# Outputs wait in the weights' staging buffers, stores go behind the loads, and the order is made anew

## The chip, the cores and the metric

The kernel runs on one core of a Trainium2 chip. The metric is the time of one execution on the device, in microseconds (us), as the median of several runs.

## The reference

Attention with a sliding window of 128 positions and 4 sink positions, for 4 batches of 8 heads, 768 positions and 64 channels a head; then a channel mix with a token shift over the 512 channels.

```python
scores = scale * np.matmul(q, k.transpose(0, 1, 3, 2))
keep = is_sink | in_window            # position < 4, or 0 <= row - column < 128
a = softmax(np.where(keep, scores, -1e9))
x = (a @ v).transpose(0, 2, 1, 3).reshape(B, S, 512)
x_prev = x shifted by one position, zeros first
xk = mu_k * x + (1 - mu_k) * x_prev
xr = mu_r * x + (1 - mu_r) * x_prev
k = np.maximum(xk @ w_k, 0)           # 512 -> 1024
out = sigmoid(xr @ w_r) * ((k * k) @ w_v)
```

## The kernel before

The 4 x 768 positions are cut into 12 blocks (u = 0 to 11) of 256 positions, three to a batch. For each block the kernel prepares q and k, attends, mixes, and runs the channel mix of the block.

- `load` brings q, k and v of a block in halves of 256 KB into three staging buffers each (`ks`, `qs`, `vs`). `load_weight` brings the five 1 MB pieces of the weights (two of w_k, one of w_r, two of w_v) into three staging buffers `w32`; in the traces their name is `w`. `cast` turns them into bfloat16 (`wk_sb`, `wr_sb`, `wv_h`).
- `prepare` casts q and k to bfloat16 (`qb`, `kb`, L533 and L540) and turns them: for early blocks by transposes on PE (L573) and an evacuation into `qt` and `kt` (L586), for later blocks by transposing DMAs (L559). v is cast into `vb` (L643).
- `attend` makes scores on PE (L718), exponentials on ACT (L772), a multiplication by the mask on DVE (L786), the products with v on PE (L805), and a reciprocal and a multiplication on DVE (L819, L822) into `x`.
- `mix` transposes `x` (L846 on PE with an evacuation at L855, or DMAs at L866 for the last blocks) into `xt`, and makes the differences `td` (L874) and the pieces of `xk` and `xr` (L885), four of each for a block, on DVE.
- `ffn` makes the key products on PE (L936, 32 for a block, which need all four pieces of `xk`), relu and square (L946 to L964), the gate (L976, L982), the value products (L994), the output `ob` on DVE (L1003) and its store (L1010).

No loop sets the order at run time. Each step is an operation with a number; the table `ORDER` lists the numbers in the order in which they are emitted, `CHOICE` says for some of them which of ACT, DVE and POOL does it, and `SLOTS` gives the place in its pool to each result. Every engine then works through its own instructions in that order, and waits where a result or a place is missing. All transfers of consequence are issued on SP's queue, in order too. A negative number in `ORDER` is a filler product on PE (L1014), which nobody reads.

Finished outputs wait in `ob`, a pool of three places, until SP has stored them.

Of the kernel before, what the change touches and what calls it, by code (L numbers as in the profile page):

```python
# [18 lines left out]
    90: "ACT", 91: "ACT", 92: "ACT", 93: "ACT", 95: "ACT", 97: "ACT", 99: "ACT", 100: "DVE",  # L19
    103: "DVE", 108: "DVE", 109: "POOL", 111: "DVE", 112: "ACT", 113: "ACT", 139: "DVE", 142:  # L20
    "DVE", 144: "DVE", 145: "DVE", 148: "DVE", 151: "DVE", 154: "DVE", 196: "POOL", 199: "POOL",
    202: "POOL", 206: "DVE", 223: "DVE", 227: "DVE", 228: "ACT", 278: "DVE", 283: "DVE", 284:
    "POOL", 287: "ACT", 288: "DVE", 300: "DVE", 309: "ACT", 313: "ACT", 320: "DVE", 356: "DVE",
    358: "POOL", 363: "POOL", 366: "ACT", 367: "ACT", 369: "DVE", 389: "ACT", 446: "DVE", 447:
    "ACT", 527: "DVE", 548: "ACT", 552: "ACT", 555: "DVE", 560: "ACT", 595: "DVE", 597: "DVE",
    600: "POOL", 602: "DVE", 605: "ACT", 606: "DVE", 628: "ACT", 636: "ACT", 677: "POOL", 681:
    "DVE", 683: "DVE", 684: "DVE", 702: "ACT", 706: "ACT", 710: "ACT", 714: "ACT", 753: "DVE",
    759: "DVE", 761: "ACT", 782: "DVE", 783: "ACT", 787: "ACT", 791: "ACT", 795: "ACT", 832:
    "DVE", 838: "ACT", 839: "ACT", 859: "ACT", 866: "DVE", 867: "ACT", 906: "POOL", 912: "DVE",
    914: "ACT", 915: "DVE", 931: "ACT", 935: "ACT", 939: "ACT", 943: "ACT", 1000: "DVE", 1004:  # L30
    "DVE", 1005: "ACT", 1008: "DVE", 1009: "ACT", 1028: "DVE", 1037: "ACT",
# [116 lines left out]
class Plan:  # L148
# [23 lines left out]
    def run(self):  # L172
        keys = [(name, key) for o in self.ops for name, key in o["take"]]
        for (name, key), slot in zip(keys, SLOTS, strict=True):
            self.buf[key] = self.pools[name][slot]
# [8 lines left out]
def kernel(  # L184
# [14 lines left out]
    nc = tc.nc  # L199
# [7 lines left out]
    NC = Dm // 128  # L207
# [6 lines left out]
    P = Plan()  # L214
# [164 lines left out]
    warm = tile1([128, 256], BF16, "warm")  # L379
# [689 lines left out]
```

## Time and profile before

| | us |
|---|---|
| median of 3 runs | 169.1 |
| lowest, highest | 167.48, 170.65 |
| the profiled execution, span | 167.6 |

The page and the trace are of one execution, whose span from first to last instruction is 167.6 us; that is near the lowest of the runs. The granted clock of PE is 1.00 in nearly all of it.

In the tables a row of a timeline is: start in us, time to the end in us, engine, source line, operation, out<-in, shapes, how many were merged; in square brackets the engine's idle time before it and what ended it. Instructions of one engine overlap at their ends, so the time of a step in a full stream is read from start to start. A row of waits is: who waited, for what, us in total, how often, the longest. Line numbers of the changed kernel are three to seven higher at the same place.

### The profile page before, as it was taken

Reading aid. Unit: us, or ns where it says so; the run is one execution under the profiler, and the core shown is the slowest. Engines: PE = TensorE matmul, PEld = TensorE weight load, DVE = VectorE, ACT = ScalarE, POOL = GpSimd, SP = SyncE. Lnnn points to the kernel's source line nnn. Section 1 sums busy time; section 2 is a strip of 40 time slices with the busy share of each in tenths; the row PEclk is TensorE's granted clock in tenths of the full one; section 3 lists DMA queues with packets and bytes.
Section 4 is the critical chain, followed back from the end, with each engine's and each line's share of the span. In section 5 each row is a group of like instructions: output and inputs, shape, how many; then the busy total and the mean of one; then the engine's idle time right before and its main releaser. Section 6 shows DMA issues by size and latency. Waiting matters only on the chain.

```text
span 167.6 us, 4210 instructions
## 1 busy us (share of the span) xinstructions
PE 159.7 (95%) x1601; PEld 102.4 (61%) x1601; DVE 146.2 (87%) x375; ACT 133.4 (80%) x221; POOL 16.6 (10%) x43
## 2 busy tenths in 40 slices
PE   6999997999999999899999999999999999999991
PEld 1447574755558576676556885665765576764850
DVE  5189999999999999899999999989798799998821
ACT  4269998999999997999879999989799829614340
POOL 6423021005000010022000000010010000000000
PEclk9999999999999999999999999999999999999999
DMA  4999989999899999979999999999997774131303
GB/s 102 300 327 369 346 172 312 372 324 328 189 248 166 204 294 224 253 153 133 218 256 149 214 239 174 233 219 200 211 189 185 194 162 155 63 66 63 125 0 125
DMA packets 79042, 34.60 MB, mean 206 GB/s; under 512 B 67112, under 2 KB 73520, under 8 KB 79024
## 3 DMA queue, kind: packets, MB, share of 16 engines
q1 hardware_dynamic: 79008, 34.35, 92.0%
q8 instruction: 12, 0.20, 0.5%
q14 instruction: 6, 0.05, 0.1%
q10 hardware_dynamic: 16, 0.00, 0.0%
HBM read 24.12 MB, written 6.29 MB: 181 GB/s over the span
## 4 chain that ended last, share of the span: by engine, by line
PE 58%; DVE 11%; DMA 11%; SPq 7%; ACT 7%; issue 3%; ACTq 0%; DVEq 0%
PE bank L936 18%; PE bank L994 18%; PE bank L976 8%; DMA vs<-in_v_dram 6%; SPq L334 5%; PE sc L718 4%; PE bank L805 4%; DMA qs<-in_q_dram 3%; ACT e L772 3%; DMA qt<-qb 2%; DVE ob L1003 2%; DVE e L786 2%; PE bank L846 2%; DVE x L822 2%; PE bank L573 2%
## 5 line engine op out<-in xcount | busy, mean ns | idle before, releaser
L936 PE MATMUL bank<-xk,wk_sb 128*128 128x256 bf16 x384 | 48.1, 273 | 0.1
L994 PE MATMUL bank<-wv_h,kk 128*128 128x512 bf16 x184 | 46.4, 379 | 0.0
L772 ACT ACTIVATE e<-sc 128x1024 bf16<-128x1024 f32 (+1 forms) x48 | 45.4, 974 | 1.2 <-PE sc L718 1.2
L936 PEld LDWEIGHTS <-wk_sb 128*128 128x128 bf16 x384 | 36.2, 98 | 7.6 <-issue 0.7
L786 DVE TENSOR_TENSOR e<-e,mask 128x1024 bf16<-128x1024 bf16 (+1 forms) x48 | 30.7, 655 | 0.7 <-ACT e L772 0.5
L946 ACT ACTIVATE rl<-bank 128x512 bf16<-128x512 f32 x38 | 22.4, 616 | 8.6 <-PE bank L936 8.5
L994 PEld LDWEIGHTS <-kk 128*128 128x128 bf16 x184 | 16.6, 98 | 14.4 <-issue 0.3
L976 PE MATMUL bank<-wr_sb,xr 128*128 128x512 bf16 x96 | 23.8, 379 | 0.0
L885 DVE SCALAR_TENSOR_TENSOR xr<-td,mu_all,xt 128x256 bf16<-128x256 bf16 x48 | 22.5, 482 | 0.0
L885 DVE SCALAR_TENSOR_TENSOR xk<-td,mu_all,xt 128x256 bf16<-128x256 bf16 x48 | 21.3, 477 | 0.1
L964 ACT ACTIVATE kk<-rl 128x512 bf16<-128x512 bf16 x26 | 16.7, 649 | 5.3 <-DVE rl L950 5.3
L822 DVE TENSOR_TENSOR x<-bank,rec 128x256 bf16<-128x256 f32 x48 | 19.2, 416 | 0.3
L1003 DVE SCALAR_TENSOR_TENSOR ob<-th,bank 128x512 f32<-128x512 f32 x23 | 15.7, 681 | 4.2 <-PE bank L994 3.3
L805 PEld LDWEIGHTS <-e 128*128 128x128 bf16 x352 | 14.4, 97 | 5.8 <-DVE e L786 1.0
L805 PE MATMUL bank<-vb,e 128*128 128x65 bf16 x352 | 16.9, 193 | 0.8 <-DVE e L786 0.8
L982 ACT ACTIVATE th<-bank 128x512 f32<-128x512 f32 x24 | 14.3, 616 | 3.6 <-PE bank L976 3.5
L1014 PE MATMUL bank<-warm 128*128 128x512 bf16 x44 | 13.8, 440 | 1.5 <-DVE warm L1032 1.1
L718 PE MATMUL sc<-qt,kt 64*128 64x128 bf16 (+1 forms) x256 | 13.9, 237 | 0.3 <-DMA qt<-qb 0.2
L976 PEld LDWEIGHTS <-xr 128*128 128x128 bf16 x96 | 8.9, 98 | 8.6
L718 PEld LDWEIGHTS <-kt 64*128 64x128 bf16 x256 | 9.3, 94 | 4.5 <-issue 3.0
L874 DVE TENSOR_TENSOR td<-xt 128x512 bf16<-128x512 bf16 x24 | 10.1, 425 | 0.8 <-ACT xt L855 0.8
L855 ACT COPY xt<-bank 128x512 bf16<-128x512 bf16 x15 | 9.1, 608 | 1.8 <-PE bank L846 1.8
(72 smaller groups left out, 157.9 us busy)
## 6 DMA issues: line engine op xcount, KB each, us to landing
vs<-in_v_dram SPq DMA_DIRECT2D x24, 256.0 KB, 5.0
ks<-in_k_dram SPq DMA_DIRECT2D x24, 256.0 KB, 5.6
qs<-in_q_dram SPq DMA_DIRECT2D x24, 256.0 KB, 5.1
out_dram<-ob SPq DMA_DIRECT2D x23, 256.0 KB, 2.9
w<-in_moe_w_k_dram SPq DMA_DIRECT2D x2, 1024.0 KB, 7.3
w<-in_moe_w_v_dram SPq DMA_DIRECT2D x2, 1024.0 KB, 8.6
w<-in_moe_w_r_dram SPq DMA_DIRECT2D x1, 1024.0 KB, 7.1
kt<-kb SPq DMA_TRANSPOSE x16, 4.1
```

Source lines behind the costliest of these rows:

```text
L718: nc.tensor.matmul(out=sc[:, a, o0:o1], lhsT=lhs[rows], rhs=rhs[rows], start=u not in BIAS, stop=True, skip_group_check=u in BIAS)
L772: nc.scalar.activation(out=buf[ek][:, :, lo:], in_=buf[sck][:, :, lo:], func=AF.Exp, scale=scale)
L786: nc.vector.tensor_tensor(out=at, in0=at, in1=m, op=ALU.mult)
L805: nc.tensor.matmul(out=o[:, g, a, :], lhsT=e[:, a, e0:e0 + 128], rhs=rhs, start=(T == 0 and i == 0), stop=(i == len(blocks) - 1), skip_gro ...
L822: P.op("DVE", dve(256), lambda ok=ok, rk=rk, c=c: nc.vector.tensor_tensor(out=buf["x", u][:, :, 128 * c:128 * c + 128].rearrange("p g (a d ...
L885: nc.vector.scalar_tensor_tensor(out=buf[key][:, c, :], in0=buf[tk][:, i, :], scalar=mu[w][:, c:c + 1], in1=xt[:, c, t0 - 1:t0 + 255], op0 ...
L936: nc.tensor.matmul(out=ps[:, i, :], lhsT=wk_sb[:, c, 128 * f:128 * f + 128], rhs=xk[:, c, :], start=(c == 0), stop=(c == NC - 1), skip_gro ...
L946: nc.scalar.activation(out=buf[rk], in_=buf[psk].rearrange("p (i t) -> p i t", i=2), func=AF.Relu)
L964: nc.scalar.activation(out=buf["kk", u][:, 2 * f2:2 * f2 + 2, :], in_=buf[rk], func=AF.Square)
L976: nc.tensor.matmul(out=buf[psk], lhsT=buf["xr", u][:, c, 128 * g:128 * g + 128], rhs=wr_sb[:, c, :], start=(c == 0), stop=(c == NC - 1))
L994: nc.tensor.matmul(out=buf[psk], rhs=wv_h[:, f, :], lhsT=buf["kk", u][:, f, 128 * g:128 * g + 128], start=(f == 0), stop=(f == NF - 1))
L1003: P.op("DVE", dve(512), lambda psk=psk, tk=tk, bk=bk: nc.vector.scalar_tensor_tensor(out=buf[bk], in0=buf[tk], scalar=1.0, in1=buf[psk], o ...
```

## The change

- The pool `ob` gets the twelve quarters of the three weight staging buffers as further places, 15 in all. In the traces an output in such a place is called `w`.
- `ORDER`, `CHOICE` and `SLOTS` are new. A filler product may have 128 columns, which the new order does not use.

```diff
+    P.pools["ob"] += [w[:, c, :] for w in P.pools["w32"] for c in range(NC)]
...
-                self.fill(self.pools["bank"][-1 - i])
+                self.fill(banks[(-1 - i) % len(banks)], 512 if -i <= len(banks) else 128)
...
 CHOICE = {
-    90: "ACT", 91: "ACT", 92: "ACT", 93: "ACT", 95: "ACT", 97: "ACT", 99: "ACT", 100: "DVE",
+    90: "POOL", 91: "POOL", 92: "POOL", 93: "POOL", 94: "POOL", 95: "POOL", 96: "ACT", 98:
...
 ORDER = (
-    4, 80, 77, 0, 81, 79, 78, 82, 1, 2, 85, 3, 112, 84, 8, -1, -2, -3, -4, -1, -2, 88, 83, 6,
+    80, 82, 83, 85, 0, 2, 77, 78, 1, 79, 100, 106, -1, -2, -3, -4, -1, -2, 88, -2, -3, -4, -2,
```

Counted over the whole program, DVE has 351 instructions instead of 375, ACT 207 instead of 222, POOL 82 instead of 43, PE 34 filler products instead of 44; all other products are the same.

The first place is SP's queue from its start to the key weights `w_76` and `w_77`, before:

```order
L304 DMA vs_73<-in_v_dram 128x8x64
L334 DMA ks_67<-in_k_dram 64x4x256 x2
L334 DMA qs_70<-in_q_dram 64x4x256 x2
L334 DMA qs_71<-in_q_dram 64x4x256
L334 DMA ks_68<-in_k_dram 64x4x256 x2
L334 DMA qs_71<-in_q_dram 64x4x256
L334 DMA qs_72<-in_q_dram 64x4x256
L304 DMA vs_73<-in_v_dram 128x8x64
L334 DMA qs_72<-in_q_dram 64x4x256
L351 DMA w_76<-in_moe_w_k_dram 128x4x512
L334 DMA ks_69<-in_k_dram 64x4x256
L351 DMA w_77<-in_moe_w_k_dram 128x4x512
```

and now (the buffers 67 to 69 are `ks`, 70 to 72 `qs`, 73 to 75 `vs`):

```order
L338 DMA qs_71<-in_q_dram 64x4x256 x2
L338 DMA ks_68<-in_k_dram 64x4x256 x2
L308 DMA vs_73<-in_v_dram 128x8x64 x2
L308 DMA vs_74<-in_v_dram 128x8x64
L338 DMA ks_69<-in_k_dram 64x4x256 x2
L338 DMA qs_72<-in_q_dram 64x4x256 x2
L308 DMA vs_74<-in_v_dram 128x8x64
L338 DMA ks_67<-in_k_dram 64x4x256 x2
L338 DMA qs_70<-in_q_dram 64x4x256 x2
L355 DMA w_76<-in_moe_w_k_dram 128x4x512
L355 DMA w_77<-in_moe_w_k_dram 128x4x512
```

Ahead of these rows now stand the four halves of `ks_67` and `qs_70` for block 0. The loads of q and k for blocks 0 to 3 and of v for blocks 0 and 1 stand ahead of the weights, where before the first weights came after 12 loads.

The second place is DVE ahead of the last piece of `xk_113`, block 0's. Before, from the reciprocal of the last attention step of block 0:

```order
L819 RECIPROCAL rec_104<-bank_63 128x4
L874 TENSOR_TENSOR td_110<-xt_155 128x512
L822 TENSOR_TENSOR x_107<-bank_63,rec_104 128x2x128
L786 TENSOR_TENSOR e_94<-e_94,mask 128x1024
L885 TENSOR_SCALAR xr_117<-td_110,mu_all,xt_155 128x256
L885 TENSOR_SCALAR xk_113<-td_110,mu_all,xt_155 128x256
L874 TENSOR_TENSOR td_111<-xt_155 128x512
L885 TENSOR_SCALAR xk_113<-td_110,mu_all,xt_155 128x256
L885 TENSOR_SCALAR xk_113<-td_111,mu_all,xt_155 128x256 x2
```

and now the end of that stretch (`x_108` is block 1's attention):

```order
L823 RECIPROCAL rec_103<-bank_66 128x4
L826 TENSOR_TENSOR x_108<-bank_64,rec_106 128x2x128
L889 TENSOR_SCALAR xk_113<-td_110,mu_all,xt_155 128x256
L826 TENSOR_TENSOR x_108<-bank_66,rec_103 128x2x128
L878 TENSOR_TENSOR td_111<-xt_155 128x512
L826 TENSOR_TENSOR x_108<-bank_65,rec_102 128x2x128
L889 TENSOR_SCALAR xk_113<-td_110,mu_all,xt_155 128x256
L878 TENSOR_TENSOR td_112<-xt_155 128x512
L889 TENSOR_SCALAR xk_113<-td_111,mu_all,xt_155 128x256 x2
```

Block 1's masks, reciprocals and all four `x_108` have moved ahead of block 0's last piece; two of its evacuations and two casts for later blocks stand there as well.

The third place is SP's queue around the last load. Before, the stores stood among the loads; now the rows from the first store on are:

```order
L1014 DMA out_dram<-ob_133 128x512
L563 DMA_TRANSPOSE qt_92<-qb_82 128x4x128
L308 DMA vs_75<-in_v_dram 128x8x64
L563 DMA_TRANSPOSE qt_92<-qb_82 128x4x128
L308 DMA vs_74<-in_v_dram 128x8x64
L870 DMA_TRANSPOSE xt_156<-x_107 128x4x128 x2
L1014 DMA out_dram<-w_76 128x512
L563 DMA_TRANSPOSE kt_85<-kb_81 128x4x128 x2
L1014 DMA out_dram<-w_78 128x512
L870 DMA_TRANSPOSE xt_156<-x_108 128x4x128 x2
L1014 DMA out_dram<-ob_134 128x512
L1014 DMA out_dram<-w_76 128x512
```

One store of 25 stands ahead of the last load (`vs_74`) where there were 15, and the rest follow it.

More of the change, by code (lines that the diff above doesn't have):

```diff
@@ L18 @@
 CHOICE = {
-    90: "ACT", 91: "ACT", 92: "ACT", 93: "ACT", 95: "ACT", 97: "ACT", 99: "ACT", 100: "DVE",
[L20 to L30, printed above, removed]
@@ L31 @@
-    "DVE", 1005: "ACT", 1008: "DVE", 1009: "ACT", 1028: "DVE", 1037: "ACT",
+    90: "POOL", 91: "POOL", 92: "POOL", 93: "POOL", 94: "POOL", 95: "POOL", 96: "ACT", 98:
+    "ACT", 99: "ACT", 100: "DVE", 103: "DVE", 106: "POOL", 108: "DVE", 109: "POOL", 113: "DVE",
+    139: "POOL", 142: "POOL", 144: "DVE", 145: "POOL", 147: "DVE", 148: "POOL", 150: "DVE", 193:
+    "DVE", 196: "POOL", 198: "DVE", 202: "DVE", 224: "ACT", 228: "ACT", 232: "ACT", 235: "DVE",
+    278: "DVE", 280: "DVE", 284: "DVE", 287: "ACT", 288: "ACT", 293: "DVE", 300: "DVE", 309:
@@ new lines @@
+    "ACT", 316: "DVE", 356: "POOL", 358: "POOL", 361: "POOL", 363: "POOL", 367: "ACT", 385:
+    "ACT", 389: "ACT", 393: "ACT", 397: "ACT", 438: "POOL", 441: "POOL", 443: "POOL", 456:
+    "DVE", 464: "DVE", 465: "ACT", 473: "ACT", 516: "POOL", 518: "POOL", 521: "POOL", 523:
+    "POOL", 526: "ACT", 548: "ACT", 560: "ACT", 595: "POOL", 597: "POOL", 600: "POOL", 602:
+    "POOL", 628: "ACT", 636: "ACT", 675: "POOL", 683: "DVE", 701: "DVE", 702: "ACT", 706: "ACT",
+    710: "ACT", 714: "ACT", 753: "POOL", 757: "POOL", 759: "POOL", 774: "DVE", 783: "ACT", 791:
@@ L32 @@
+    "ACT", 795: "ACT", 830: "POOL", 834: "DVE", 836: "POOL", 838: "DVE", 855: "ACT", 859: "ACT",
+    863: "ACT", 906: "DVE", 910: "POOL", 912: "POOL", 931: "ACT", 935: "ACT", 943: "ACT", 996:
+    "DVE", 997: "ACT", 1001: "ACT", 1009: "ACT", 1025: "ACT", 1029: "ACT", 1033: "ACT", 1036:
+    "DVE",
 }
@@ L175, in run @@
             self.buf[key] = self.pools[name][slot]
+        banks = self.pools["bank"]
         for i in ORDER:
             if i < 0:
-                self.fill(self.pools["bank"][-1 - i])
+                self.fill(banks[(-1 - i) % len(banks)], 512 if -i <= len(banks) else 128)
             else:
@@ L1012, in ffn, with zeros @@
             P.op("SP", 400.0, store, rank, hold=[bk], reads=[bk], service=800.0)
-    P.fill = lambda bank: nc.tensor.matmul(out=bank, lhsT=warm[:, 0:128], start=True,
-                                           rhs=warm.unsqueeze(1).to_broadcast([128, 2, 256]),
-                                           stop=True)
+    def zeros(bank, n):
+        nc.tensor.matmul(out=bank[:, 0:n], lhsT=warm[:, 0:128], start=True, stop=True,
+                         rhs=warm.unsqueeze(1).to_broadcast([128, 2, 256]) if n == 512 else
+                         warm[:, 0:n])
+    P.fill = zeros
     prepare(0, 0)
```

160 rows, old and new, of tables (ORDER, SLOTS) are left out of this document.

## The prediction

> **What bounds the kernel now.** I read the page's busy lines first, then busy time in chosen stretches, then the waits, then the timelines of PE, DVE and POOL around the place where PE stops waiting. The stretches: in each cell the busy time, the number of instructions in brackets.
>
> ```profile
> span 167.6 us, 4210 instructions
> PE 159.7 (95%) x1601; PEld 102.4 (61%) x1601; DVE 146.2 (87%) x375; ACT 133.4 (80%) x221; POOL 16.6 (10%) x43
> 2.00:10.00 8.00, 7.71 (x38) 3.33 (x37) 3.23 (x13) 3.07 (x6) 4.77 (x16) 1.00 0.96 282
> 10.00:20.00 10.00, 9.81 (x120) 6.04 (x119) 9.21 (x26) 8.99 (x14) 1.96 (x4) 1.00 1.09 353
> 20.00:28.30 8.30, 6.98 (x82) 4.57 (x80) 8.17 (x20) 7.61 (x13) 1.93 (x3) 1.00 0.96 239
> 28.30:163.70 135.40, 134.21 (x1365) 88.12 (x1363) 123.92 (x312) 113.13 (x191) 7.16 (x14) 1.00 0.94 194
> ```
>
> The columns after the first are PE, PEld, DVE, ACT, POOL, then the granted clock, the DMA share and GB/s. From 28.3 to 163.7 us PE is busy 134.21 of 135.40 us. Busy alone says little, so the waits of PE in that stretch, and two places of its timeline:
>
> ```profile
> PE bank L693 <- ACT rl L946: 0.6, 1, 0.6
> PE sc L718 <- DMA qt<-qb: 0.2, 1, 0.2
> 1.13 2.74 PE L1014 MATMUL bank<-warm 128*128 128x512 bf16 x6 [1.13 <-DVE warm L1032]
> 18.33 0.62 PE L718 MATMUL sc<-qt,kt 64*128 64x256 bf16 x12
> 18.88 0.40 PE L573 MATMUL bank<-ident,qb 128*128 128x128 bf16 x4
> 19.43 0.40 PE L573 MATMUL bank<-ident,qb 128*128 128x128 bf16 x4
> 19.66 0.81 PE L1014 MATMUL bank<-warm 128*128 128x512 bf16 x3
> 21.41 2.78 PE L936 MATMUL bank<-xk,wk_sb 128*128 128x256 bf16 x24
> 24.13 0.29 PE L760 MATMUL bank<-vsink,es 64*128 64x130 bf16 x4
> 28.31 0.39 PE L573 MATMUL bank<-ident,kb 128*128 128x128 bf16 x4
> ```
>
> The first two rows are all of PE's waits for others after 28.3: 0.8 us in 135, one of them for a load. From start to start the 24 key products take 24.13 - 21.41 = 2.72 us (0.113 each), a score group of 12 takes 18.88 - 18.33 = 0.55, four transposes 19.66 - 19.43 = 0.23. So PE is a full stream from 28.3 on, and nothing that makes loads or other engines faster shortens it by more than the 1.2 us it is not busy. The losses lie ahead of 28.3, where PE mostly fills time:
>
> ```profile
> 0.00:28.30 28.30, 13.77 (x44) 4.23 (x44) 1.00 0.94 275
> ```
>
> That is the row of the filler products (L1014) alone: 13.8 us busy. What this opening waits for is DVE, whose timeline ends in the mixing of the first block:
>
> ```profile
> 6.43 0.43 DVE L540 CAST kb<-ks 128x512 bf16<-128x512 f32 x1 [3.01 <-DMA ks<-in_k_dram]
> 8.59 0.43 DVE L540 CAST qb<-qs 128x512 bf16<-128x512 f32 x1 [1.66 <-DMA qs<-in_q_dram]
> 9.54 0.68 DVE L586 COPY kt<-bank 128x512 bf16<-128x512 bf16 x1
> 10.14 0.68 DVE L586 COPY qt<-bank 128x512 bf16<-128x512 bf16 x1
> 10.80 0.76 DVE L540 CAST kb<-ks 128x512 bf16<-128x512 f32 x2
> 12.04 0.56 DVE L786 TENSOR_TENSOR e<-e,mask 128x768 bf16<-128x768 bf16 x1 [0.48 <-ACT e L772]
> 14.92 0.37 DVE L819 RECIPROCAL rec<-bank 128x4 f32<-128x4 f32 x2
> 15.20 0.72 DVE L822 TENSOR_TENSOR x<-bank,rec 128x256 bf16<-128x256 f32 x2
> 15.84 0.55 DVE L786 TENSOR_TENSOR e<-e,mask 128x768 bf16<-128x768 bf16 x1
> 18.17 0.69 DVE L786 TENSOR_TENSOR e<-e,mask 128x1024 bf16<-128x1024 bf16 x1
> 18.78 0.48 DVE L885 SCALAR_TENSOR_TENSOR xr<-td,mu_all,xt 128x256 bf16<-128x256 bf16 x1
> 19.57 0.42 DVE L874 TENSOR_TENSOR td<-xt 128x512 bf16<-128x512 bf16 x1
> 19.91 1.27 DVE L885 SCALAR_TENSOR_TENSOR xk<-td,mu_all,xt 128x256 bf16<-128x256 bf16 x3
> 21.10 0.48 DVE L885 SCALAR_TENSOR_TENSOR xr<-td,mu_all,xt 128x256 bf16<-128x256 bf16 x1
> ```
>
> The last xk piece ends at 19.91 + 1.27 = 21.18, the first key product starts at 21.41. From 9.54 on DVE hardly rests.
>
> **The change part by part.** *Stores behind loads.* 15 of the 25 stores stood ahead of the last load, now one does. They leave a queue that PE does not wait for, so I take 0; at best it is the 1.2 us above. The other side: 24 stores now come late. They have some 40 us with this DMA load:
>
> ```profile
> 130.00:163.70 33.70, 33.47 (x282) 21.36 (x280) 28.08 (x67) 16.88 (x29) 0.00 (x0) 1.00 0.37 102
> ```
>
> There 102 GB/s is moved and 353 was possible (the row of 10 to 20 us): 33.7 us hold 11.9 MB at that rate, and the 24 stores with 6.3 MB fit beside the transposes. The end itself (sixteen products of L906, two DVE steps, two stores) is unchanged, so the last 4 us stay.
>
> *Weights later.* On SP's queue 16 half loads of q and k and four of v now go ahead of the key weights.
>
> ```profile
> ks<-in_k_dram SPq DMA_DIRECT2D x24, 256.0 KB, 5.6
> w<-in_moe_w_k_dram SPq DMA_DIRECT2D x2, 1024.0 KB, 7.3
> ```
>
> 20 times 0.262 MB and 1.05 MB are 6.3 MB. By 10 us 8 x 282 = 2.26 MB have moved; the remaining 4.0 MB at 353 GB/s take 11.4 us, so the first half of the key weights is there at about 21.4 us, 22.4 with the transfers that run beside it. Its cast now stands on POOL, which has no such cast in the trace: a cast of half its size takes POOL 0.62 us (row of 24.46, below), so 1.2 us by doubling, 0.69 if it ran like a DVE step of 1024, and 1.6 if it ran like two stretched ones (0.81). I take 1.2, POOL's own row: the first key weights are ready at 23.6 us.
>
> *When the key products start.* They also need the last xk piece of block 0, and DVE now does most of block 1's attention ahead of it. Against before, the order puts ahead of that piece: one cast more (0.33, the step from 0.43 to 0.76 for two), two evacuations of transposes more (0.60 from 9.54 to 10.14), one evacuation into xt less (about a cast, 0.33), three masks of 1024 more (0.61 from 18.17 to 18.78), four reciprocals (0.14 from 14.92 to 15.20 for two), four x (0.32 from 15.20 to 15.84 for two), one td (0.34 from 19.57 to 19.91), one xr less (0.40, as 21.10 - 19.91 for three). Sum: 0.33 + 1.20 - 0.33 + 1.83 + 0.56 + 1.28 + 0.34 - 0.40 = 4.8 us. DVE's rests change too. Before it waited 3.01, 1.66 and 0.48 us, 5.2 in all. Now 1.7 us of its memsets stand behind q's cast and no longer fill the wait for k (4.6 us instead of 3.0); q is there earlier (0.7 instead of 1.66); between kt's evacuation at about 10.1 and the first mask at about 11.6 it has nothing (1.4 instead of 0.48). That is 6.7: 1.5 us more. The last xk piece ends at 21.2 + 4.8 + 1.5 = 27.5 us, later than the weights, and the key products start at 27.7 without any disturbance. If DVE finds work in those rests it is 26.2.
>
> *What that is worth.* At 28.31 PE's unbroken stream began before. Ahead of its first key product the new order has, against what PE had done by 28.31: five groups of four transposes more (5 x 0.23), two score groups of 12 more (2 x 0.55), 24 key products less (2.72). It is 0.5 us of work behind, so a start at 27.8 would give the old end. 27.7 gives -0.1; 26.2 gives -1.6.
>
> *Block 1's keys.* 16 key products (16 x 0.113 = 1.8 us) follow; then those of block 1, which need its last xk piece. Between the two last pieces DVE has six L885 steps and one td, 6 x 0.40 + 0.34 = 2.7 us. PE waits 0.9 us, where the order holds three filler products: +0.9.
>
> *POOL beside DVE.* DVE goes from 375 to 351 instructions, ACT from 222 to 207, POOL from 43 to 82: 33 casts of 512 and the six casts of key and gate weights. In the 28.3 to 163.7 stretch DVE's relief (24 times 0.43 to 0.69, 10 to 17 us) meets a PE that does not wait: 0. What it costs is seen at 24.5 us:
>
> ```profile
> 24.54 0.81 DVE L885 SCALAR_TENSOR_TENSOR xr<-td,mu_all,xt 128x256 bf16<-128x256 bf16 x1
> 25.27 1.09 DVE L786 TENSOR_TENSOR e<-e,mask 128x1024 bf16<-128x1024 bf16 x1
> 24.46 0.62 POOL L540 CAST kb<-ks 128x512 bf16<-128x512 f32 x1
> 25.02 0.81 POOL L643 CAST vb<-vs 128x512 bf16<-128x512 f32 x1
> ```
>
> The xr step takes 0.81 instead of 0.48, the mask 1.09 instead of 0.69, each begun while POOL casts, and POOL's second cast is stretched as well. The Trainium skill ("SBUF - State Buffer", Who interferes with whom) says that the port pair these engines share is an exclusive lock: a DVE step with two SBUF inputs and a GpSimd step that reads SBUF block each other for the whole instruction. By that rule alone two weight casts ahead of the start would cost DVE up to their whole length; the trace agrees that a step waits, but with 0.33 and 0.40 us lost against casts of 0.62 and 0.81. Between 22.4 and 27.5 us POOL has two of the six weight casts, 2.4 us, while DVE does masks, td and xk; the other four follow up to some 31 us. Bounds from these rows: 0, if they fall beside DVE's steps from PSUM, and 2.4 before the start plus up to 2.4 before block 1's keys. I take one loss of 0.4 a cast and a little for the longer hold, 1.0 us in all.
>
> Sum: -0.1 + 0.9 + 1.0 = +1.8 us, 167.6 + 1.8 = 169.4 us for an execution like the profiled one. That one lies 1.5 us under the runs' median of 169.1 (0.9%), and I carry the ratio: 169.4 x 169.1 / 167.6 = 170.9 us, 1.1% slower. About 2% is what a measurement of this kernel can tell from no change.
>
> **The rivals.** *Faster: the keys start with the weights.* If DVE's new work fits into its rests (it had 5.2 us of them) and POOL's casts miss it, the first key product starts at 23.6 us, 4.2 ahead of 27.8: 163.4, or 164.9 us as a median. For it: ACT and DVE have less to do in sum. Against it: DVE's sum above, and that the rests lie in the first 12 us, before k, q and the scores are there.
>
> *Slower: the lock.* If all six weight casts (6 x 1.2 = 7.2 us) stand in DVE's way instead of 1.0, while DVE sets PE's pace, it is 167.6 - 0.1 + 0.9 + 7.2 = 175.6, or 177.2 us. Place: 22 to 32 us, DVE's masks and L885 steps. It decides beyond a loss of 2.6 us. For it: the two stretched rows, and that these casts come one behind the other. Against it: half of DVE's steps there read PSUM, and the xr step of 0.81 lost less than a cast's length.
>
> *The loads do bring it.* Without the stores PE's 1.2 us and the lock's 1.0 vanish: 167.6 - 0.1 + 0.9 - 1.2 = 167.2, or 168.7 us. For it: a DMA share of 0.94 and more. Against it: one load wait of 0.2 us on PE.
>
> *Slower: a cold PE.* 34 filler products stand in place of 44. The first six fillers took 2.74 us, 0.46 each, twice the 0.226 of two key products, which are half as wide: if rests drop PE to that pace once more for about 5 us ahead of the keys, 3 us of work double: 169.4 + 3 = 172.4, or 173.9 us. The granted clock reads 1.00 through all rows, and I see little for it. The Trainium skill ("TensorE: Matmul & The Clock Gate", What's actually happening) has the clock fall to half after one idle window of about 3.4 us; no run here shows that yet.
>
> **How the numbers follow.** The forecast (DVE-bound start, small lock loss) gets 0.44, the loads 0.14; both are within 2%: 0.58. The start with the weights 0.12: faster. The lock 0.23 and the cold PE 0.07: slower, 0.30. The range reaches from the start at 26.2 with no lock loss and no later waits (167.6 - 1.6 - 1.2 = 164.8, 166.3 as a median; I take 166.0) to nearly the full lock, 176.5.
>
> **What would show it.** Right: the first L940 product at 27 to 29.5 us; DVE without a rest over 0.5 us from 16 us on; a wait of about 1 us between block 0's and block 1's keys; POOL's weight casts at 22 to 31 us with DVE steps of 0.7 us and more beside them; after that a PE with under 2 us of waits, and DMA idle for long stretches before 100 us. Wrong: a start before 25 us, or waits of PE after 40 us that add to more than 2 us, above all for POOL's casts by way of SP's transposes.

## The result and the profile after

The changed kernel takes 177.49 us in the median of four runs (176.21 to 178.27), the kernel before 169.88 on the same chip. The ratio is 1.051, 95% interval 1.040 to 1.063: slower. Forecast were 170.9 us and a range of 166.0 to 176.5. Some executions of a kernel are slower as a whole, at a lower granted clock; medians below are of all runs, ratios leave the slow ones out. The profiled execution took 177.45 us, with a span of 175.7 against 167.6 before. A run's time is 1.7 us more than its span throughout, so the profile before, at 167.6 + 1.7 = 169.3 us, was one of middling speed and not near the lowest. From the page of the changed kernel, the span and the busy line, and from busy time in chosen stretches (columns PE, PEld, DVE, ACT, POOL, granted clock, DMA share, GB/s):

```profile
span 175.7 us, 4190 instructions
PE 160.3 (91%) x1591; PEld 102.3 (58%) x1591; DVE 148.2 (84%) x351; ACT 127.2 (72%) x206; POOL 49.6 (28%) x82
28.30:34.00 5.70, 2.94 (x23) 2.06 (x23) 5.59 (x7) 2.41 (x4) 5.17 (x5) 1.00 0.94 266
34.00:40.00 6.00, 4.41 (x27) 3.41 (x27) 5.28 (x11) 2.98 (x5) 0.87 (x2) 0.74 1.07 352
57.00:63.00 6.00, 6.00 (x59) 3.57 (x57) 5.62 (x17) 4.44 (x10) 0.00 (x0) 1.00 0.05 14
69.00:80.00 11.00, 9.90 (x111) 6.81 (x110) 10.79 (x23) 8.77 (x13) 7.23 (x10) 1.00 1.14 211
```

Right behind 28.3 us, where PE was full before, it works half of the time, and from 34 to 40 us at a granted clock of 0.74. DVE is busy in 5.59 of 5.70 us there with only seven instructions. DVE's busy time as a whole rose by 2.0 us, although it has 24 instructions fewer. The timelines of PE, DVE and POOL at this place:

```profile
27.62 0.27 PE L940 MATMUL bank<-xk,wk_sb 128*128 128x256 bf16 x1
28.59 0.38 PE L940 MATMUL bank<-xk,wk_sb 128*128 128x256 bf16 x2 [0.70 <-DVE xk L889]
29.77 1.14 PE L940 MATMUL bank<-xk,wk_sb 128*128 128x256 bf16 x9 [0.80 <-DVE xk L889]
35.59 6.08 PE L940 MATMUL bank<-xk,wk_sb 128*128 128x256 bf16 x39 [3.27 <-DVE xk L889]
...
26.04 0.92 DVE L889 SCALAR_TENSOR_TENSOR xk<-td,mu_all,xt 128x256 bf16<-128x256 bf16 x1
26.89 1.25 DVE L878 TENSOR_TENSOR td<-xt 128x512 bf16<-128x512 bf16 x1
28.07 2.82 DVE L889 SCALAR_TENSOR_TENSOR xk<-td,mu_all,xt 128x256 bf16<-128x256 bf16 x3
31.21 1.26 DVE L889 SCALAR_TENSOR_TENSOR xk<-td,mu_all,xt 128x256 bf16<-128x256 bf16 x1
32.39 1.25 DVE L889 SCALAR_TENSOR_TENSOR xr<-td,mu_all,xt 128x256 bf16<-128x256 bf16 x1
34.43 1.11 DVE L889 SCALAR_TENSOR_TENSOR xk<-td,mu_all,xt 128x256 bf16<-128x256 bf16 x2
...
25.53 2.33 POOL L508 CAST wk_sb<-w 128x1024 bf16<-128x1024 f32 x2 [5.43 <-DMA w<-in_moe_w_k_dram]
28.24 2.38 POOL L508 CAST wk_sb<-w 128x1024 bf16<-128x1024 f32 x2 [0.38 <-DMA w<-in_moe_w_k_dram]
31.15 2.22 POOL L508 CAST wr_sb<-w 128x1024 bf16<-128x1024 f32 x2 [0.53 <-DMA w<-in_moe_w_r_dram]
```

The key products start at 27.62 us and wait at once for pieces of `xk`: 0.70, 0.80 and 3.27 us. Beside each of POOL's six weight casts (1.0 to 1.2 us) one DVE step takes 1.25 us in place of 0.42 to 0.48 (0.92 beside the first). Summed over the six steps, DVE loses 4.4 us. This is what is called the lock below: a DVE step that reads two operands from SBUF, such as these, stands still while POOL casts. Block 1's last piece of `xk` is the end of the last DVE row, 35.54 us; the 39 products follow at once.

To see where time is lost in the whole program I added up PE's work. Every product but the fillers counts with its width at the key products' pace at full clock (0.108 us for 256 columns, half of that where it has 64 rows, a quarter where it has 32 columns of weights). Each kernel has some 135.6 us of such work. The table gives the time in us at which so much of it was done, worked out from each trace; the kernels behind the second are those of the experiments.

| work done | before | changed | casts on ACT | fillers | loads first | casts spread, loads first |
|---|---|---|---|---|---|---|
| 8 | 24.69 | 26.53 | 26.48 | 26.59 | 27.06 | 27.29 |
| 10 | 29.08 | 30.80 | 30.02 | 30.60 | 31.02 | 30.83 |
| 12 | 31.55 | 36.90 | 33.47 | 36.76 | 38.31 | 33.49 |
| 14 | 33.63 | 40.64 | 35.63 | 38.90 | 40.81 | 36.47 |
| 20 | 39.86 | 47.19 | 44.52 | 45.84 | 47.65 | 43.02 |
| 42 | 63.75 | 70.77 | 68.28 | 69.33 | 71.34 | 66.79 |
| 48 | 71.04 | 79.33 | 77.08 | 77.98 | 78.56 | 73.76 |
| 90 | 116.08 | 124.34 | 122.38 | 123.70 | 123.88 | 119.20 |
| 132 | 160.21 | 168.95 | 166.95 | 168.33 | 169.20 | 164.61 |

The changed kernel is 7.0 us behind at 14 us of work (40.6 us). It stays there to 70.8 us, loses 1.3 us more by 79.3, and ends 8.1 us behind (at 132 us of work it is 8.7; the last few us of the program give some of that back). The second loss has its origin on SP's queue, in the row of its waits and the two POOL rows that follow it in time:

```profile
SPq L563 <- ACT es L704: 12.7, 3, 10.5
69.82 1.59 POOL L544 CAST qb<-qs 128x512 bf16<-128x512 f32 x2 [13.81 <-DVE w L1007]
71.36 1.07 POOL L537 CAST kb<-ks 128x512 bf16<-128x512 f32 x1
```

From about 54 to 63.6 us SP stands in front of a transposing DMA; DMA moves 14 GB/s from 57 to 63 us. The loads behind land from 70 us on, and POOL then casts 7.23 us out of 11 while PE waits 1.1 us.

### The profile page after: what moved, and what is told of

Same layout as the page of the kernel before. It is cut to its first block, busy times and chain, and to the rows that moved or that the text cites. A ratio compares the mean times of both kernels' runs of the same rounds, so it can differ in the third digit from the quotient of the medians.

```text
span 175.7 us, 4190 instructions
## 1 busy us (share of the span) xinstructions
PE 160.3 (91%) x1591; PEld 102.3 (58%) x1591; DVE 148.2 (84%) x351; ACT 127.2 (72%) x206; POOL 49.6 (28%) x82
## 4 chain that ended last, share of the span: by engine, by line
PE 51%; DVE 27%; DMA 5%; ACT 5%; issue 4%; SPq 3%; POOL 2%; DVEq 0%; ACTq 0%; POOLq 0%
PE bank L940 17%; PE bank L998 14%; PE bank L980 8%; DVE xk L889 5%; DVE x L826 4%; DVE e L790 4%; PE bank L809 4%; PE sc L722 4%; DVE td L878 3%; DMA ks<-in_k_dram 3%; SPq L338 3%; DVE xr L889 2%; DMA xt<-x 2%; ACT rl L950 2%; ACT kk L968 2%
## 5 line engine op out<-in xcount | busy, mean ns | idle before, releaser
L940 PE MATMUL bank<-xk,wk_sb 128*128 128x256 bf16 x384 | 49.6, 279 | 4.8 <-DVE xk L889 4.8
L998 PE MATMUL bank<-wv_h,kk 128*128 128x512 bf16 x184 | 44.6, 379 | 0.8 <-DVE w L1007 0.4
L950 ACT ACTIVATE rl<-bank 128x512 bf16<-128x512 f32 x42 | 24.9, 599 | 15.6 <-PE bank L940 14.8
L790 DVE TENSOR_TENSOR e<-e,mask 128x1024 bf16<-128x1024 bf16 (+1 forms) x48 | 32.9, 697 | 1.2 <-ACT e L776 1.1
L889 DVE SCALAR_TENSOR_TENSOR xk<-td,mu_all,xt 128x256 bf16<-128x256 bf16 x48 | 25.8, 565 | 0.3
L968 ACT ACTIVATE kk<-rl 128x512 bf16<-128x512 bf16 x33 | 20.7, 631 | 0.5
L647 POOL CAST vb<-vs 128x512 bf16<-128x512 f32 x17 | 12.6, 743 | 25.9 <-DMA vs<-in_v_dram 17.8
L544 POOL CAST qb<-qs 128x512 bf16<-128x512 f32 x12 | 9.4, 794 | 26.7 <-DVE w L1007 13.8
L1019 PE MATMUL bank<-warm 128*128 128x512 bf16 x34 | 12.1, 455 | 1.2 <-DVE warm L1039 1.1
L1007 DVE SCALAR_TENSOR_TENSOR w<-th,bank 128x512 f32<-128x512 f32 x16 | 10.9, 679 | 2.0 <-PE bank L998 1.9
```

Of the source, the lines that this page charges most:

```text
L790: nc.vector.tensor_tensor(out=at, in0=at, in1=m, op=ALU.mult)
L889: nc.vector.scalar_tensor_tensor(out=buf[key][:, c, :], in0=buf[tk][:, i, :], scalar=mu[w][:, c:c + 1], in1=xt[:, c, t0 - 1:t0 + 255], op0 ...
L940: nc.tensor.matmul(out=ps[:, i, :], lhsT=wk_sb[:, c, 128 * f:128 * f + 128], rhs=xk[:, c, :], start=(c == 0), stop=(c == NC - 1), skip_gro ...
L950: nc.scalar.activation(out=buf[rk], in_=buf[psk].rearrange("p (i t) -> p i t", i=2), func=AF.Relu)
L968: nc.scalar.activation(out=buf["kk", u][:, 2 * f2:2 * f2 + 2, :], in_=buf[rk], func=AF.Square)
L998: nc.tensor.matmul(out=buf[psk], rhs=wv_h[:, f, :], lhsT=buf["kk", u][:, f, 128 * g:128 * g + 128], start=(f == 0), stop=(f == NF - 1))
```

## The experiments

The kernel's operations are named by their numbers in `ORDER` and `CHOICE`: 90 to 93 are the casts of the key weights, 94 and 95 those of the gate's.

**The casts back on ACT** (a1).

```diff
 CHOICE: 90 to 95
-POOL
+ACT      # and in ORDER behind ACT's steps 215, 283, 227 and 309
```

> The changed kernel with its six casts of key and gate weights on ACT, as in the kernel before, in place of POOL; PE, DVE and SP keep their order. Theory A (POOL's weight casts hold DVE: in the trace of after one DVE step per cast takes 1.25 us in place of 0.42 to 0.48, 4.4 us in all between 25.5 and 33.4 us, and PE then waits 3.3 us for block 1's last xk piece and runs its next 39 products at a lower granted clock): DVE's steps there are 0.48 again, the 3.3 us wait is under 1 us, and the time falls by 3.5 to 5.5 us, to 172 to 174 us. Rival B (the loss is the longer list of DVE steps ahead of block 1's keys, and weights that land 3 us later): the wait stays at 2 us or more, the time falls by less than 1.5 us.

Measured: 176.63 us, ratio to before 1.046 (1.040 to 1.052). DVE's and PE's timelines:

```profile
26.73 1.27 DVE L889 SCALAR_TENSOR_TENSOR xk<-td,mu_all,xt 128x256 bf16<-128x256 bf16 x3
29.76 0.88 DVE L889 SCALAR_TENSOR_TENSOR xk<-td,mu_all,xt 128x256 bf16<-128x256 bf16 x2
32.05 4.61 PE L940 MATMUL bank<-xk,wk_sb 128*128 128x256 bf16 x40
37.78 1.02 PE L980 MATMUL bank<-wr_sb,xr 128*128 128x512 bf16 x4 [1.12 <-ACT qt L590]
39.71 1.89 PE L980 MATMUL bank<-wr_sb,xr 128*128 128x512 bf16 x8 [0.91 <-ACT rl L950]
```

Three pieces of `xk` take 1.27 us, not 2.82; block 1's last piece ends at 30.64 us, not 35.54, and the products that started at 35.59 start at 32.05, at full clock. At 14 us of work the lag is 2.0 us in place of 7.0. So the mechanism is shown, but the time fell by 0.9 us only, which the intervals do not tell from nothing: ACT, busy for 132.4 us in place of 127.2, made PE wait 1.12 and 0.91 us between 36.7 and 39.7 us, and at 20 us of work the lag is 4.7 us again. The time expected from theory A was wrong because I priced ACT's side at nothing.

**The casts on POOL in the kernel before**, all six (b1) and those of the key weights alone (b2).

```diff
 CHOICE of the kernel before
-    90: "ACT", 91: "ACT", 92: "ACT", 93: "ACT", 95: "ACT",
+    90: "POOL", 91: "POOL", 92: "POOL", 93: "POOL", 94: "POOL", 95: "POOL",    # b2: 90 to 93 only
```

> The kernel before with the same six weight casts on POOL (five of them were ACT's, one DVE's); nothing else moved. Theory A: six DVE steps between 17 and 33 us lose about 0.77 us each, 4.6 us; what falls ahead of the key products' start (two or three casts) and what follows up to 28 us is seen by PE: 2 to 4.5 us slower, 172 to 174 us. Rival B (the casts cost nothing where DVE's order is the old one and the weights are early): within 1 us of the kernel before, or faster, as ACT has 5.6 us less to do.

> The kernel before with the four casts of key weights alone on POOL, the gate's two as they were. With all six on POOL PE lost 1.6 us for good at 29.9 to 32.2 us, beside the gate's casts, and nearly nothing beside the key's (they met DVE's steps from PSUM, and DVE had just ended the pieces that PE waits for). Place decides: within 0.5 us of the kernel before. Each cast costs DVE, and so the time, the same: 1 us slower.

Measured: b1 170.58 us, 1.015 (1.007 to 1.023); b2 170.21 us, 1.010 (1.005 to 1.014). First b1, POOL, PE and DVE, then b2, DVE and PE:

```profile
21.67 2.88 POOL L504 CAST wk_sb<-w 128x1024 bf16<-128x1024 f32 x1 [2.82 <-DMA w<-in_moe_w_k_dram]
24.61 1.05 PE L936 MATMUL bank<-xk,wk_sb 128*128 128x256 bf16 x8 [1.26 <-POOL wk_sb L504]
29.65 2.83 DVE L885 SCALAR_TENSOR_TENSOR xk<-td,mu_all,xt 128x256 bf16<-128x256 bf16 x3
```

```profile
20.75 2.07 DVE L885 SCALAR_TENSOR_TENSOR xk<-td,mu_all,xt 128x256 bf16<-128x256 bf16 x3
22.48 2.85 PE L936 MATMUL bank<-xk,wk_sb 128*128 128x256 bf16 x23 [1.49 <-DVE xk L885]
```

Both kernels lose where a cast meets pieces of `xk`: 2.83 and 2.07 us for three in place of 1.27. In b1 one cast was itself held for 2.88 us by DVE's steps, and PE waited for it. The six casts cost 1.5% here (0.7 to 2.3%, 1.1 to 3.8 us), at the low end of my 2 to 4.5 us. Likely that is because the key products' start is earlier and DVE has other steps beside them; no run isolates it. My expectation for b2, within 0.5 us, was wrong: it is 1% or 1.6 us slower, as the other guess had it, and in its trace a cast fell on the last pieces. In b1's trace the first cast starts at 16.63 us in place of 17.25 and the third at 21.67 in place of 20.72, and they met other steps. So it takes little to change which step is hit; how far this differs from run to run, one trace of each kernel does not show.

**The clock** (a2): fillers in the place of the wait.

```diff
 ORDER ahead of 314, the first product of block 1's keys
-    -2, -2, -2, 314,
+    -2, -2, -2, -2, -2, -2, -2, -2, -2, -2, -2, -2, -2, -2, -2, -2, -2, 314,
```

> The changed kernel with 14 more filler products in front of block 1's keys, 14 x 0.22 = 3 us of PE work that nobody needs, put into the 3.3 us in which PE waits there. Theory C (the lower granted clock after that wait, 0.87 in the mean of 28.3 to 40 us and 0.152 us for each of 39 key products in place of 0.113, costs 39 x 0.04 = 1.5 us of its own): the clock stays 1.00, and the time falls by 1 to 1.5 us. Rival D (DVE, not PE, sets the pace up to 43 us, and PE has room): no change, within 0.5 us.

Measured: 176.86 us, 1.050 (1.044 to 1.056). The fillers and the products behind them, and then the clock of the changed kernel without fillers, in stretches around the slow products:

```profile
31.20 3.83 PE L1019 MATMUL bank<-warm 128*128 128x512 bf16 x17
35.45 4.49 PE L940 MATMUL bank<-xk,wk_sb 128*128 128x256 bf16 x39 [0.31 <-DVE xk L889]
```

```profile
36.00:36.90 0.90, 0.90 (x11) 0.80 (x9) 0.90 (x2) 0.00 (x0) 0.00 (x0) 1.00 1.04 398
36.90:40.30 3.40, 3.40 (x19) 2.42 (x17) 2.71 (x7) 3.14 (x5) 0.00 (x0) 0.50 1.11 317
40.30:42.00 1.70, 1.70 (x15) 1.34 (x14) 1.23 (x4) 0.72 (x2) 0.00 (x0) 0.99 1.21 291
```

Without the fillers PE runs at half clock for 3.4 us, beginning 1.3 us after the wait's end; that costs 1.7 us. With them the 39 products take 4.49 us in place of 6.08, and the lag at 14 us of work is 5.3 us. In the time only 0.6 us of it is left, which the intervals do not tell from nothing: by the table 0.4 us is given back by 20 us of work and 0.7 more between 48 and 90. The clock's price shows in the changed kernel's own four runs too. Three have a mean granted clock of 0.99, which is one such stretch (half of 3.4 us is 1% of 175), and took 177.45 to 178.27 us; the fourth, at 0.999, took 176.21.

**The loads ahead of SP's waiting transposes** (a3), and both together (a6).

```diff
 ORDER, SP's part
-    49, 437, 442, 44, 41, 42, 39, 50, 40,
+    49, 44, 41, 42, 39, 50, 437, 442, 40,
```

> The changed kernel with five loads (halves of q, k and v of blocks 5 to 7) put ahead of the two transposes of block 5's k on SP's queue. There SP waits from 54 to 63.6 us, DMA idles for some 6 us, and the loads behind land at 70 us, so that eight POOL casts run at 69.8 to 78 us, where PE loses about 2 us. Theory E (that late bunch costs the 2 us): the loads land by 62 us, POOL casts where PE has no wait, and the time falls by 1 to 2 us. Rival A alone (each cast costs DVE the same wherever it stands, and PE's 2 us turn up at another place): within 0.7 us.

> The changed kernel with POOL's weight casts kept, the 14 filler products ahead of block 1's keys and the five loads ahead of SP's waiting transposes. If clock (1.7 us at 40 us) and bunched loads (1.2 us at 70 to 78 us) are losses of their own beside the lock, PE's lag behind the kernel before is 5.3 us at 42 us and grows by less than 1 us after that: 174 to 175 us. If the fillers' gain is given back where POOL casts later (as at 90 to 96 us with the fillers alone): 176 us or more.

Measured: a3 176.81 us, 1.048 (1.043 to 1.053); a6 177.24 us, 1.053 (1.049 to 1.056). Stretches of a3, then DVE, POOL and PE of a6:

```profile
57.00:63.00 6.00, 6.00 (x60) 3.76 (x59) 5.63 (x17) 4.43 (x9) 2.38 (x4) 1.00 1.18 249
69.00:80.00 11.00, 10.91 (x131) 7.97 (x128) 10.64 (x26) 9.79 (x16) 3.60 (x6) 1.00 0.91 187
```

```profile
61.59 1.58 DVE L889 SCALAR_TENSOR_TENSOR xk<-td,mu_all,xt 128x256 bf16<-128x256 bf16 x2
62.85 1.55 POOL L537 CAST kb<-ks 128x512 bf16<-128x512 f32 x2
65.47 0.38 PE L940 MATMUL bank<-xk,wk_sb 128*128 128x256 bf16 x2 [1.10 <-DVE xk L889]
```

In a3 the idle DMA is gone and PE loses nothing from 69 to 80 us, as theory E has it; the time gains 0.7 us at best, which is what rival A gave. In a6, where PE is 1.7 us earlier, the same casts fall beside another block's pieces of `xk` (two take 1.58 us, not 0.87), and PE waits 1.10 us there. So the expected sum did not come: a bunch of POOL casts that is moved finds another DVE step.

**The casts spread** (a4), and with the loads first (a5).

```diff
 CHOICE: 90 to 95
-POOL
+90, 91, 93: ACT; 92, 94, 95: DVE      # each at or beside a rest of its engine
```

> The changed kernel with its six weight casts spread over engines that have room there: three on ACT, the second half's first one and both gate casts on DVE, each in or next to a rest that DVE has when POOL does not cast; ACT's exponential and square of that place behind the last of them. With all six on ACT the 3.3 us wait of PE was gone, but PE then waited 2.35 us for ACT, 37 to 40 us. Theory A (the lock, and the slow clock that its 3.3 us wait brings, are the loss up to 42 us; only the place of ACT's casts ate the gain): PE's work up to 42 us lags behind the kernel before by 1 to 2.5 us, not 7, and the time falls by 4 to 5.5 us, to 172 to 173.5 us. Rival F (the longer DVE list and the late weights bind there anyway, whichever engine casts): the lag stays over 4 us, the time falls by under 2 us.

> The kernel with the six weight casts spread over ACT and DVE, and with the five loads ahead of SP's two waiting transposes as well. Theory A with E (the two losses are apart, the loads' one worth about 1.2 us at 70 to 78 us): 1 to 1.5 us faster than with the casts alone, about 171 us, 1 to 1.5% behind the kernel before. Rival (PE's gain there is given back by the casts of a later place, at 90 to 96 us): no faster than with the casts alone.

Measured: a4 174.96 us, 1.039 (1.032 to 1.046); a5 173.42 us, 1.030 (1.025 to 1.034), the row of 28.3 to 40 us of a5 beside that of the changed kernel (the second):

```profile
28.30:40.00 11.70, 10.43 (x76) 7.06 (x75) 11.66 (x25) 10.99 (x18) 2.08 (x4) 1.00 0.97 296
```

```profile
28.30:40.00 11.70, 7.35 (x50) 5.48 (x50) 10.87 (x17) 5.38 (x9) 6.04 (x6) 0.87 1.01 310
```

PE works 10.43 us there, not 7.35, at full clock. The two edits together take back 4.1 of the 7.6 us between the medians. The loads' edit has 1.5 us of it, though the intervals of a4 and a5 touch. a4 came out between its two theories: PE's lag at 14 to 20 us of work is 3.3 to 3.7 us (A: 1 to 2.5, F: over 4), and the time fell by 2.5 us (A: 4 to 5.5, F: under 2). So the lock is a large part of the loss in the opening, but the longer DVE list or the late weights bind there too. One of a4's four runs, the traced one, also has a stretch at half clock, from 22.1 to 25.5 us, and took 176.06 us; the others took 173.8 to 175.6.

**POOL's late casts** (a9): from a5, two of them moved to ACT.

```diff
 CHOICE, ORDER
-    914 (v), 910: "POOL" (k), both of block 11
+    914: "ACT", 910: "ACT", behind 706
```

> The kernel with the weight casts spread and the five loads ahead of SP's transposes, and now with two of POOL's late casts (halves of v and k of block 11, 119.7 to 121.1 us there) on ACT, in a rest of 1.2 us that ACT has just behind. Beside them two DVE steps took 0.83 us in place of 0.48, and PE's lag grew by 1.2 us between 119 and 126 us. If those casts make that lag: 0.7 to 1.2 us faster, about 172.5 us. If it has another cause there (DVE is full in that place, with or without POOL): within 0.4 us.

Measured: 172.77 us, 1.022 (1.014 to 1.029), against a5 some 0.8% or 1.3 us less by the ratios. The intervals overlap and the opening of its profiled execution was 1 us quicker than a5's, so this does not settle it.

**More POOL casts in the kernel before** (b3).

```diff
                 self.ops[i]["emit"]()
+                for name in self.ops[i]["writes"]:
+                    if name[0] == "th":
+                        nc.gpsimd.tensor_copy(out=spare, in_=self.buf[name])
```

> The kernel before with 24 more POOL casts that nobody reads (128x512, f32 to bf16, each from a sigmoid-part tile th as soon as ACT has written it, into a spare tile), from 36 us on, two by two over the stretch in which PE hardly waits. This is what 24 of the changed kernel's casts of q, k and v do to DVE, without the relief. If each costs a DVE step some 0.4 us as at other places, DVE gets 6 to 9 us more to do in the 135 us, where it rests 11.5 us: DVE's busy time 152 to 155 us, and the time 1 to 4 us longer where those casts meet a step that PE waits for. If POOL's casts cost nothing in the full stretch (my 0): within 0.8 us.

Measured: 170.32 us, 1.010 (1.002 to 1.018), from its page and its groups:

```profile
PE 160.0 (95%) x1601; PEld 102.1 (61%) x1601; DVE 149.8 (89%) x375; ACT 133.7 (80%) x221; POOL 35.8 (21%) x67
L1018 POOL CAST spare<-th 128x512 bf16<-128x512 f32 x24 | 18.5, 771 | 100.1 <-ACT th L985 99.8
```

DVE's busy time rose from 146.2 to 149.8 us, 0.15 us a cast. Many casts meet steps that read PSUM, and those lose nothing: 16 such steps run beside the casts (`ob`, `rec`, `x`, `rl`, `vsink`) and are longer than the like before by 0.1 us in all, while 30 steps that read SBUF alone lose 4.6 us; two of these are casts of q with one operand, which lose 0.4 us each. The sum is less than the 6 to 9 us expected, but it is not free: 24 casts cost some 1.7 us of time, 1% (0.2 to 1.8%), in a stretch in which PE hardly waited.

**Casts cut in half** (a8).

```diff
-            return lambda: engine.tensor_copy(out=out, in_=buf[key][cut])
+            # on POOL: two tensor_copy, each of half the columns
```

> The changed kernel with each of POOL's six weight casts cut into two of half the size (12 of 128x512). If a DVE step waits for the whole POOL instruction that stands in its way, and POOL then for it, each half costs about 0.4 us in place of 0.78 for a whole one: the same sum, PE waits for block 1's keys for 3 us as now, and the time stays within 1 us. If long instructions are what hurts (DVE gets in between short ones without loss): DVE's steps lose under 0.2 us each, PE's wait falls under 1.5 us, the time by 2 us or more.

Measured: 176.25 us, 1.043 (1.035 to 1.052). DVE and PE:

```profile
26.41 2.33 DVE L896 SCALAR_TENSOR_TENSOR xk<-td,mu_all,xt 128x256 bf16<-128x256 bf16 x3
33.29 6.08 PE L947 MATMUL bank<-xk,wk_sb 128*128 128x256 bf16 x39 [2.68 <-DVE xk L896]
```

Each of the shorter casts takes about 0.35 us from a DVE step, which makes 0.83 of 0.48. From the start of block 0's second piece to the end of block 1's last DVE needs 7.99 us, with whole casts 9.50 and in a1 4.64. So cutting takes the loss from 4.9 to 3.4 us; most of it stays, though POOL's casts now take 9.5 us in sum in place of 7.1. The wait is 2.68 us, not 3.27, and the half clock comes after it just the same. The time is 1.2 us less between the medians, with intervals that overlap. Neither guess is met: the number of steps that are hit counts, and so does the length of a cast.

**The stores** among the loads again (a7, from a5), and stores late alone (b4, from the kernel before).

```diff
 a7: ORDER, 14 stores
-    behind the last loads
+    40 steps behind the step that fills the place
 b4: the kernel before
+    P.pools["ob"] += [w[:, c, :] for w in P.pools["w32"] for c in range(NC)]
-    15 stores ahead of the last load
+    2 stores ahead of it, SLOTS of ob from 0 to 14 in turn
```

> The kernel with the weight casts spread over ACT and DVE and the five loads ahead of SP's transposes, and now 14 of its stores put back among the loads, each some 40 steps of the written order behind the step that fills its place; the 15 places stay. Theory (the order of stores and loads is worth nothing, since PE waits for no load or store): within 0.8 us of the kernel without this edit, about 173.4 us. Rival G (late stores are a gain of their own, up to the 1.2 us that PE was not busy before): 1 us or more slower. Rival H (25 stores late are a cost, at the end): 1 us faster.

> The change's own idea alone: the kernel before, with its engine choices and its order of loads, casts and products, but with the 15 places for finished outputs, and 14 of the 15 stores that stood ahead of the last load moved behind it. My term for this was 0, at best -1.2 us (all of PE's waits after 28.3 us). Theory (the stores' move is worth next to nothing and costs nothing; the loss is in the choices and orders made anew): within 0.8 us of the kernel before. Rival G (stores that wait for their filler hold the loads and transposes behind them on SP, 16.5 us of waits there in the kernel before; without them it is faster): 1 us or more faster. Rival H (the stores, all late, run into the end): 1 us or more slower.

Measured: a7 176.14 us, 1.041 (1.032 to 1.050), against a5's 1.030; b4 168.21 us, 0.999 (0.995 to 1.002). PE at the place in a7 where it stands longest, and two stretches of it:

```profile
71.47 0.82 PE L722 MATMUL sc<-qt,kt 64*128 64x128 bf16 x10 [2.66 <-DMA kt<-kb]
68.50:71.40 2.90, 0.31 (x4) 0.10 (x2) 2.61 (x9) 0.59 (x1) 0.00 (x0) 0.88 0.84 144
71.40:77.60 6.20, 6.13 (x40) 3.13 (x42) 2.62 (x7) 3.30 (x5) 1.73 (x3) 0.50 1.06 191
```

a7 is 1.1% slower than a5 by the ratios, whose intervals just touch. Of the three guesses only rival G fits, but the cause stays open. In its trace PE waits for a transposing DMA that SP issued from 66.5 to 69.3 us, behind two stores; in a5 no store stands there, and SP had issued the transposes by 65.3 us. That a store which waits for its output holds them is my guess: SP's longest wait for an output, 5.5 us, is at the end of the program, and at this place SP's wait of 1.8 us is put down to a cast of POOL. The half clock does not explain the time either. The traced execution took 179.38 us at a mean granted clock of 0.978; three others ran at 1.00 and still took 175.3 to 176.1 us, where a5 took 172.8 to 174.0. b4 is the clean test: the change's idea alone neither gains nor costs anything within 0.5%.

## Why the prediction was wrong, step by step

- **Stores behind loads, 0: right** (b4).
- **Key weights at 23.6 us: wrong, without effect on the start.** They landed at 25.5 us, not 22.4, and the first cast was done at 26.7. DVE's last piece was still later. But the six casts moved with them, from the 22.4 to 31 us that I had in mind to 25.5 to 33.4, where DVE has `td`, `xk` and `xr` steps one behind the other and none from PSUM from 26.1 us on. How much of the lock's price this is was not isolated.
- **Start of the key products, 27.7 us and -0.1: right for DVE's order alone, and by luck in the changed kernel.** The forecast lets the start wait for block 0's last piece of `xk`, at 27.5 us. In a1, without POOL's casts, that piece ends at 27.60, so the sum over DVE's steps was right. In the changed kernel it ends at 29.71. What starts at 27.62 is a product that needs the first piece alone; those that need the last start at 29.77. By work, 8.65 us of it was done at 27.62 us. The kernel before had 9.31 us done at 28.31, so the start alone is worth -0.03 us.
- **Block 1's keys, +0.9: right in size, as far as a1 tells.** There block 1's last piece ends at 30.64 us. From 27.66, 16 products and four transposes in a full stream would end at 27.66 + 1.81 + 0.23 = 29.70, 0.9 us sooner. The 0.62 us that a1's PE does wait there are for ACT.
- **POOL's lock, +1.0: the step that failed.** I took one loss of 0.4 us a cast "and a little for the longer hold", from rows of casts half as long. Measured is a loss of nearly the whole rest of the cast, 0.77 to 0.84 us for five of the six and 4.4 us in sum, all of it on the chain from DVE to PE, which waits 0.70, 0.80 and 3.27 us. At 14 us of work the lag is 5.3 us without the slow clock (a2) and 2.0 without the lock (a1), so at least 3.3 us are the lock's; a1's 2.0 us hold waits of 0.32, 0.37 and 0.62 us for ACT that the changed kernel does not have. The rule that I weighed, of the Trainium skill ("SBUF - State Buffer", Who interferes with whom), has the loser blocked for the whole instruction; the rows agree with it (the `td` step of 26.89 ends 0.3 us behind POOL's cast) and not with my 0.4.
- **Clock, 0: wrong.** Half clock came, as the rival of the cold PE (0.07) had it, but at another place and as a consequence of the lock: 3.4 us at half clock, 1.7 us lost. Without that wait the clock stayed at 1.00 in the traced executions of a1, a2 and a5; two of a1's other runs and one of a2's have 0.99. The Trainium skill ("TensorE: Matmul & The Clock Gate", What's actually happening) has half clock after an idle window of 3.4 us; here waits of 3.27 (the changed kernel), 2.68 (a8) and 2.66 us (a7) were enough, and shorter ones in a4 and b2 (below). The forecast also read too much into the clock's column: it shows 1.00 from the start, but in the trace before the fillers start 0.42 us apart up to 6.43 us and 0.22 us apart from 6.82 on, and the first record of the clock is at 6.77. The slow first fillers were half clock.
- **Relief of DVE and no loss after 40 us, 0: wrong by 1.1 to 1.5 us.** It came close to a sign that I had named, PE's waits after 40 us of over 2 us by way of SP's transposes: they are 1.9 us, all of them for DVE. SP's transposes held loads, the loads came in a bunch, and POOL's casts held DVE (a3 takes this away and with it the loss from 69 to 80 us). DVE's 10 to 17 us of relief were eaten, its busy time rose.

With the measured sizes the sum reads -0.03 + 0.9 + 3.3 + 1.7 + 1.3 = 7.2 us of the 8.1; with all 4.4 us that DVE lost in place of 3.3 it is 8.3. So the parts explain the loss to within 1 us, and the lock's share is known as 3.3 to 4.4 us. The rival "the lock" gave 177.2 us, and 177.49 were measured. Its place and its mechanism were right, but that the number fits is luck: its 7.2 us for the lock stand for lock, clock and late loads together.

What stays open: a5 is still 3% behind the kernel before. By the table it loses 1.8 us by 10 us of work, 1 us more by 14, and 1.2 us between 119 and 126 us. The order of the opening, with more of DVE's attention ahead of the first keys, is the likely cause of the first two. It was not isolated. No version beat the kernel before; b4 is level with it.

## What to carry to other kernels

Before you move work from one engine to POOL, list DVE's steps that read SBUF alone and will run beside it (those with two operands above all; in b3 casts lost time too), and price each POOL cast there at its own length, not at what one earlier overlap cost. If such a DVE step feeds PE, price the wait too, and what PE's clock does after it. In a queue that is worked through in order, look at what stands behind each instruction that waits: a transpose that came too early held SP for 10.5 us here, and the bunch of loads that followed collided elsewhere.

## What the runs showed of the hardware that was not expected

- The clock changes on a grid. In six traces it falls to half, at 36.90 (the changed kernel), 35.62 (a3), 22.05 (a4), 70.72 (a7), 34.22 (a8) and 29.70 us (b2). The first record of full clock in the same traces is at 6.18, 4.90, 4.99, 5.87, 6.92 and 5.80 us. The distances are 9, 9, 5, 19, 8 and 7 times 3.413 us, and half clock lasts one such step, two in a7. So the fall does not follow the wait at a fixed distance: it comes 1.31 us after work has resumed in the changed kernel and 0.18 us before that in a3. The start of the grid differs between executions; that this is why one run of a kernel has the stretch and the next has not is likely, but not shown.
- It takes no long wait. In a4 PE was busy for 2.17 us of the 3.41 us ahead of the fall, its longest wait there 0.93 us. In b2 it waited 1.49 us, worked 4.5 us, and waited again, in the first row below:

```profile
26.85:28.13 1.28, 0.00 (x1) 0.01 (x1) 1.28 (x4) 0.28 (x1) 0.69 (x1) 1.00 0.92 280
28.13:29.75 1.62, 1.40 (x18) 0.74 (x18) 1.62 (x8) 0.41 (x1) 0.00 (x0) 0.98 0.98 340
29.75:33.20 3.45, 3.42 (x28) 2.32 (x26) 3.41 (x10) 3.08 (x6) 0.00 (x0) 0.51 1.04 374
```

  A single wait of 1.26 us in b1, and two of 1.12 and 0.91 us in a1, left the clock at 1.00. How much of a step has to be idle these runs do not tell: in b2 PE was busy 1.91 us both in the step ahead of the fall (26.28 to 29.70 us) and in an earlier one (19.46 to 22.87) that no fall followed.
- The lock works both ways: a POOL cast of 1.04 us took 2.88 us (b1, 21.67) while DVE's steps came one behind the other.
